# A fused attention and MLP kernel: batch 0 with its scores in sixteens and without filler matmuls, and TensorE in a written-out order from batch 1 on

## The chip, the cores and the metric

The kernel runs on one NeuronCore of a Trainium2 chip. The metric is device time in microseconds (us) of one execution. Seven runs of the kernel before gave a median of 268.73 us (268.46 to 270.62).

The core has five engines that run beside each other and wait for one another by semaphores: TensorE (PE: matmuls, with the weight loads shown as PEld), VectorE (DVE), ScalarE (ACT), GpSimd (POOL) and SyncE (SP). POOL and SP also issue most DMAs. Matmuls write to PSUM; DVE and ACT empty it.

## The reference

For each of 4 batches and 8 heads, a sorting matrix P (8 x 8) mixes the 8 blocks of 96 rows of k and v; each block of q then attends to its own mixed block. The result x (768 x 512 for a batch) goes through a residual MLP with affine norms.

```python
for _ in range(5):                                  # P: (4, 8, 8, 8)
    P = np.exp(P - np.max(P, axis=-1, keepdims=True))
    P = P / (np.sum(P, axis=-1, keepdims=True) + 1e-09)
    P = P / (np.sum(P, axis=-2, keepdims=True) + 1e-09)
k_sorted = np.einsum('bhij,bhjcd->bhicd', P, k_b)   # v_sorted likewise
scores = scale * np.matmul(q_b, k_sb.transpose(0, 1, 2, 4, 3))
attn = softmax(scores)
x = heads side by side of np.matmul(attn, v_sb)     # (4, 768, 512)
a1 = alpha1 * x + beta1
u = x + lam * np.einsum('ts,bsd->btd', w_tok, a1)
a2 = alpha2 * u + beta2
out = u + lam * (np.maximum(a2 @ w_ch1, 0.0) @ w_ch2)
```

## The kernel before

**Stages.** Everything is unrolled. First come five rounds of the normalisation of P on ACT and DVE (lines 234 to 253), with `spin` matmuls on TensorE beside them: products of the identity that nothing reads. Then batch 0's attention with a code of its own, and the transposed token weights (`sort_wtok`, `prep_wtok`). Then for each batch the token mixing (`moe_a`: `tok_part`, `moe_tok`, `moe_turn`) and the MLP in two halves of 384 rows: `moe_h` (16 hidden tiles of 4 matmuls 128x384, ReLU on ACT) and `moe_ch` (three row tiles of 16 matmuls 128x512, then two DVE operations and two stores). A batch's MLP runs beside the next batch's attention.

**Batch 0** (lines 681 to 722). `mix_v0` and `mix_k0` make a head pair's mixed v and k (12 matmuls each, copied out in a part of four and a part of two, one by ACT and one by DVE); `turn_v0` transposes v into `Vs[0]`; `sc0` makes eight score matmuls for half a head pair and one exponential; `pv0` makes 12 matmuls with the values, a reciprocal and a product on DVE. Most `sc0` and the last two `pv0` begin with one or two `spin` matmuls. In this stage every engine keeps the order in which the code issues (`Engine.fixed`).

**Later batches.** `mix_v` and `mix_k` mix v and k for all heads; v takes a trip through DRAM (`vscr`) into `Vs[b % 2]`. `emit_scores` and `emit_pv` work by head pairs h4 = 0 to 3. From line 740 on TensorE and ACT, and from 743 DVE, aren't fixed: a planner puts the instructions in order by priority and a modelled time, except for the piece at lines 759 to 765.

**Buffers.** PSUM pool psA has 2 buffers of two banks (scores, values and mixes of the later batches), psB 4 buffers of one bank (all the rest). The hidden tiles lie in `hTa` and `hTb`, one buffer each for both halves. `ost` (output rows) has 2 buffers, `kT` 2.

**Queues.** POOL issues, in this order: q, v, k of batch 0, the token weights, the affine vectors, `W1p`, v of batch 1, `W2p`, then `prep_affine` and the additions of `moe_start`, then k and q of batch 1. At most eight of its DMAs are under way: the ninth waits for the first to land. SP issues the v trip, the transposes of q (`cross_q`, from batch 2 on) and of u (`moe_turn`, from batch 1 on), and the stores.

Of the kernel before, what the change touches and what calls it, by code (L numbers as in the profile page):

```python
# [16 lines left out]
def kernel(  # L17
# [73 lines left out]
    def const(shape, dtype, name):  # L91
        return wts.tile(shape, dtype, name=name, tag=name)

    ident16 = const([128, 128], F16, "ident16")
    pool.memset(ident16[:], 0.0)
    pool.affine_select(
        out=ident16[:], in_=ident16[:], compare_op=ALU.not_equal, fill=1.0, base=0,
        pattern=[[-1, 128]], channel_multiplier=1,
    )
    ident32 = const([128, 128], FT, "ident32")  # L100

# [7 lines left out]
    def load_raw(b, kv):  # L109
        src = (k, v)[kv]  # L110
        if b == 0:
            raw = att.tile([128, H, 6, D], F16, name=f"raw{kv}", tag=f"raw{kv}", bufs=2)
            for hh in range(2):
                pool.dma_start(
                    raw[:, hh * 4:(hh + 1) * 4, :, :],
                    src[b, hh * 4:(hh + 1) * 4].rearrange("h (p x) d -> p h x d", x=6),
                )
            raw_of[(b, kv)] = raw
            return
        raw = att.tile([128, HB * D], F16, name=f"raw{kv}", tag=f"raw{kv}", bufs=2)  # L120
        for th in range(2):
            pool.dma_start(
                raw[th * 64:(th + 1) * 64, :],
                src[b].rearrange("h (j th t) d -> th (h j) (t d)", j=NB, th=2)[th],
            )
        raw_of[(b, kv)] = raw

    qn_of = {}
    qT_of = {}

    def load_q(b):
        qT_of[b] = att.tile([128, H4, NT, 128], F16, name="qT", tag="qT", bufs=2)
        if b < 2:
            qn = att.tile([128, H, NT, D], F16, name="qn1", tag="qn", bufs=1)
            n = (4, 2)[b]
            for hh in range(n):
                hs = slice(hh * H // n, (hh + 1) * H // n)
                pool.dma_start(qn[:, hs, :, :], q[b, hs].rearrange("h (p kt) d -> p h kt d", kt=NT))
            qn_of[b] = qn
            return  # L140
# [16 lines left out]
    load_q(0)  # L157
    load_raw(0, 1)
    load_raw(0, 0)
    ones16 = const([128, 1], F16, "ones16")  # L160
    pool.memset(ones16[:], 1.0)
    dve.tensor_copy(ident32[:], ident16[:])
    NV = 2
    Vs = []
    for n in range(NV):
        t_ = const([BLK, H * NB, GRP], F16, f"Vs_{n}")
        dve.memset(t_[:, :, D:GRP], 1.0)
        Vs.append(t_)
# [8 lines left out]
    ab2 = att.tile([2 * CT, 128], FT, name="ab2", tag="sel", bufs=2)  # L177
# [3 lines left out]
    pool.dma_start(ab2[0:CT, :], moe_alpha2.rearrange("(c p) -> c p", p=128))  # L181
    pool.dma_start(ab2[CT:2 * CT, :], moe_beta2.rearrange("(c p) -> c p", p=128))
# [13 lines left out]
    def mask(n):  # L196
        if n == 0:
            dve.tensor_reduce(mskj[:], ident16[:].rearrange("p (b j) -> p j b", j=NB), AXX, ALU.add)
# [8 lines left out]
        else:  # L207
            for th in range(2):
# [25 lines left out]
    for it in range(5):  # L234
# [16 lines left out]
        if it > 2:  # L251
            turn_q(0, it - 3, act.copy)
    spin(psb([128, 512], FT, "spin_ps")[:], 7)

    def load_weights():
        for g in range(4):
            pool.dma_start(W1p[:, :, g * 512:(g + 1) * 512], w1v[:, :, g * 512:(g + 1) * 512])
        load_raw(1, 1)
        for g in range(4):
            pool.dma_start(W2p[:, g * 4:(g + 1) * 4, :], w2v[:, g * 4:(g + 1) * 4, :])  # L260
# [40 lines left out]
    def mixing_heads():  # L301
# [10 lines left out]
        for hh in range(2):  # L312
            hs = slice(hh * 4, hh * 4 + 4)
            dve.tensor_tensor(
                bigH[:, hs, :, :],
                rep[:, hs, :].unsqueeze(3).to_broadcast([128, 4, NB, 16]),
                mskt[:].unsqueeze(1).unsqueeze(1).to_broadcast([128, 4, NB, 16]),
                ALU.mult,
            )

# [6 lines left out]
    def mix_v(b, banks=2, groups=range(6), copies=(act.copy, dve.tensor_copy, act.copy)):  # L327
# [5 lines left out]
        for n in groups[::banks]:  # L333
# [19 lines left out]
    def mix_k(b, share=(4, 0, 4), gs=range(3)):  # L353
        raw = raw_of[(b, 0)]
        rhs = bigP[b][:].rearrange("p g i -> p (g i)")
        if b not in kT_of:
            kT_of[b] = att.tile([128, H4 * NB, BLK], F16, name="kT", tag="kT", bufs=2)
# [17 lines left out]
    def mix_heads(kv, h4, out, copies):  # L375
# [3 lines left out]
        for (lo, hi), copy in zip(((0, 4), (4, 6)), copies):  # L379
# [8 lines left out]
            copy(dst[:, lo:hi], mps[:].rearrange("p t (i r) -> p t i r", r=16))  # L388

    def mix_k0(h4):  # L390
        if 0 not in kT_of:
            kT_of[0] = att.tile([128, H4 * NB, BLK], F16, name="kT", tag="kT", bufs=2)
        mix_heads(0, h4, kT_of[0][:, h4 * NB:(h4 + 1) * NB, :], (act.copy, dve.tensor_copy))
# [3 lines left out]
    def mix_v0(h4):  # L397
        vT0.append(moep.tile([128, NB, BLK], F16, name=f"vT_{h4}", tag="u32", bufs=9))
        mix_heads(1, h4, vT0[h4][:], (dve.tensor_copy, act.copy))
# [12 lines left out]
    def emit_scores(b, h4, g, spins=0):  # L412
        kT = kT_of[b]
        qT = qT_of[b]
        blocks = ((0, 1, 2, 6), (3, 4, 5, 7))[g] if b == 0 else range(4 * g, 4 * g + 4)
        sps = psa([128, 2, 4, 128], FT, "sc_ps")
        spin(sps[:, 0, :, :].rearrange("p i x -> p (i x)"), spins)
        for ii, i in enumerate(blocks):
            for h2 in range(2):
                rows = slice(h2 * 64, (h2 + 1) * 64)  # L420
                pe.matmul(
                    sps[0:BLK, h2, ii, 0:BLK], kT[rows, h4 * NB + i, :], qT[rows, h4, :, i * 16:(i + 1) * 16],
                    start=True, stop=True,
                )
        et = att.tile([BLK, 2, 4, BLK], F16, name="et", tag="et", bufs=4)
# [35 lines left out]
    def pv_tiles(h4, g, et, spins=0):  # L461

        bank = psb([128, 4, 128], FT, "x_ps")[:].rearrange("p a x -> p (a x)")
        spin(bank, spins)
        xps = bank[:, 0:6 * GRP].rearrange("p (a i g) -> p a i g", i=3, a=2)
        flat = et[:].rearrange("p a i x -> p (a i x)")
        for rows, i in ((slice(0, 128), 0), (slice(BLK, 128), 3)):
            for h2 in range(2):
                for ii in range(3):
                    vi = 3 * g + ii if i == 0 else 6 + g  # L470
                    at = (h2 * 4 + ii) * BLK
                    lhsT = flat[:, at:at + 128] if i == 0 else et[:, h2, 3, 32 * ii:32 * ii + 32]
                    pe.matmul(
                        xps[rows, h2, ii, 0:D + 1], lhsT, Vs[0][:, (2 * h4 + h2) * NB + vi, 0:D + 1],
                        start=True, stop=True,
# [8 lines left out]
    def emit_attention(b):  # L484
        x128 = moep.tile([128, NT, C], F16, name="x128", tag="x128", bufs=2)
        xs = moep.tile([BLK, 2, C], F16, name="xs", tag="xs", bufs=1)
        x_of[b] = x128

        def gather(lo, hi):
            for a in range(3):  # L490
                dve.tensor_copy(x128[96:128, a:a + 4:3, lo:hi], xs[32 * a:32 * a + 32, :, lo:hi])

        prev = [emit_scores(b, 0, g) for g in range(2)]
        for h4 in range(1, H4):
            cur = [emit_scores(b, h4, g) for g in range(2)]
            emit_pv(b, h4 - 1, prev, x128, xs)
            prev = cur
            if h4 == H4 - 1:
                gather(0, 384)
        emit_pv(b, H4 - 1, prev, x128, xs)  # L500
        gather(384, C)


# [5 lines left out]
    def sort_wtok(n):  # L509
# [3 lines left out]
        for lo, hi, base in ((0, 96, 0), (96, 128, TAIL)):  # L513
            w = hi - lo
            dve.tensor_copy(
# [122 lines left out]
    def moe_h(b, hf, which=range(HT)):  # L638
        if (b, hf) not in hT_of:
            hTa = moep.tile([128, 12, 384], BF, name="hTa", tag="big", bufs=1)  # L640
            hTb = moep.tile([128, HT - 12, 384], BF, name="hTb", tag="hTb", bufs=1)
            hT_of[(b, hf)] = [hTa[:, m, :] if m < 12 else hTb[:, m - 12, :] for m in range(HT)]
        for m in which:
# [6 lines left out]
            act.activation(hT_of[(b, hf)][m], hps[:], AF.Relu)  # L650

    def moe_ch(b, hf, kks=range(3)):
        hT = hT_of[(b, hf)]
        for kk in kks:
# [3 lines left out]
            for lo, hi in ((0, 384), (384, C)) if last else ((0, C),):  # L658
                cps = psb([128, hi - lo], FT, "ch_ps")
                for m in range(HT):  # L660
# [3 lines left out]
                    )  # L664
                dve.tensor_tensor(cps[:], cps[:], lamB[:, lo:hi], ALU.mult)
# [4 lines left out]
                )  # L670

# [3 lines left out]
    def sc0(h4, g, spins=0):  # L675
        ets[(h4, g)] = emit_scores(0, h4, g, spins)

    def pv0(h4, g, spins=0):
        pv_tiles(h4, g, ets[(h4, g)], spins)

    x_of[0] = moep.tile([128, NT, C], F16, name="x128", tag="x128", bufs=2)
    mixing_heads()
    turn_q(0, 2, act.copy)
    mix_v0(0)
    turn_q(0, 3, act.copy)
    for h4 in range(1, H4):
        mix_v0(h4)
    load_weights()
    turn_v0(0, dve.tensor_copy)
    mix_k0(0)  # L690
    mix_k0(1)
    sc0(0, 0, 1)
    turn_v0(1, dve.tensor_copy)
    sc0(0, 1, 1)
    mix_k0(2)
    pv0(0, 0)
    sc0(1, 0, 1)
    turn_v0(2, dve.tensor_copy)
    pv0(0, 1)
    sc0(1, 1, 1)  # L700
    mix_k0(3)
    pv0(1, 0)
    sc0(2, 0, 1)
    sort_wtok(0)
    pv0(1, 1)
    sc0(2, 1, 1)
    sort_wtok(1)
    prep_wtok(range(1), dve.tensor_copy)
    pv0(2, 0)
    sort_wtok(2)  # L710
    sc0(3, 0)
    prep_wtok(range(1, 2), dve.tensor_copy)
    pv0(2, 1)
    sc0(3, 1)
    prep_affine()
    turn_v0(3, act.copy)
    prep_wtok(range(2, 4), act.copy)
    pv0(3, 0, 2)
# [3 lines left out]
    pv0(3, 1, 2)  # L722
# [5 lines left out]
    load_raw(1, 0)  # L728
    load_q(1)
# [18 lines left out]
    moe_h(0, 0, range(5))  # L748
    for n in range(6):
        moe_h(0, 0, range(5 + n, 6 + n))  # L750
# [5 lines left out]
    moe_h(0, 0, range(11, HT))  # L756
    moe_turn(0, 1)
    stack.close()
    pe.fixed = True
    for kk in range(2):  # L760
        moe_ch(0, 0, (kk,))
        mix_k(1, gs=((0, 1), (2,))[kk])
        for h4 in range(2 * kk, 2 * kk + 2):
            turn_q(1, h4, dve.tensor_copy)
    pe.fixed = False
    for b in range(1, B):
        if b > 1:
            if b > 2:
                cross_q(b)
            mixing_matrices(b)  # L770
            mix_v(b)
            if b == 2:
                opened = pool.tensor_copy(gate[:], Vs[0][0:1, 0, 0:2])
                with tc.issue_after(opened.ins):
                    load_q(3)
                    load_raw(3, 1)
                    load_raw(3, 0)
            mix_k(b)
        emit_attention(b)
        if b == 1:  # L780
            moe_ch(0, 0, (2,))
        else:
            moe_h(b - 1, 0)
            moe_ch(b - 1, 0)
        moe_h(b - 1, 1)
        moe_a(b)
        moe_ch(b - 1, 1)
# [3 lines left out]
    for hf in range(2):  # L791
        moe_h(B - 1, hf)
        moe_ch(B - 1, hf)
# [30 lines left out]
```

The softmax here doesn't subtract the row's maximum and nothing guards it: scores larger than these inputs give would overflow.

## Time and profile before

| | |
|---|---|
| median of 7 runs | 268.73 us |
| profiled execution, its own time | 268.85 us |
| its span, first to last instruction | 267.1 us |
| mean granted TensorE clock | 0.998 |
| PE, DVE, ACT, POOL busy | 97%, 58%, 47%, 35% |
| first mixing matmul of batch 0 | 13.10 us |
| first `tok_ps` matmul of batch 0 | 33.97 us |
| first `tok_ps` matmul of batches 1 and 2 | 85.59 us, 144.37 us |

Times within the profile count from the start of the span. A row of the timeline merges instructions of a kind: its start, the stretch that they take, engine, line, operation, output and inputs, shape, and count. All lines read L65, since one helper issues everything; tiles tell the instructions apart. A matmul's end is modelled and overlaps the next one's start, so the pace of TensorE is read from one row's start to the next row's start. "x_ps" are the products with the values, "sc_ps" the scores, "m_ps", "k_ps" and "v_ps" the mixes, "vt_ps" and "q_ps" the transposes of v and q.

### The profile page before, as it was taken

How to read it: one execution, taken by the hardware profiler on the slowest of the kernel's cores; microseconds unless marked ns; L12 is line 12 of the kernel's file. 1: busy time of each engine (PE TensorE's matmuls, PEld its weight loads, DVE VectorE, ACT ScalarE, POOL GpSimd, SP SyncE). 2: the span in 40 equal slices, each digit the busy share in tenths (PEclk: the TensorE clock that was granted, in tenths of full speed). 3: DMA queues.
4: the chain of work that ended last, by engine and by line, in shares of the span. 5: the costliest groups of instructions: out<-in, count | busy, mean ns of one | idle time of the engine just before them, and what ended most of it. 6: DMA issues, size and time to landing. Idle time of an engine off the chain costs nothing.

```text
span 267.1 us, 5149 instructions
## 1 busy us (share of the span) xinstructions
PE 258.6 (97%) x2049; PEld 141.6 (53%) x2059; DVE 154.6 (58%) x333; ACT 125.8 (47%) x232; POOL 92.7 (35%) x100
## 2 busy tenths in 40 slices
PE   7899999999999999999999999999999999999993
PEld 2467745566555444554565444654565445545542
DVE  5878778629567866632675957714585962042033
ACT  3376757643585312880375414970475305604600
POOL 8523689203675624008817225002409000000000
PEclk9999999999999999999999999999999999999999
DMA  5999999999999543499999442495200332012012
GB/s 76 176 208 255 207 212 206 210 214 109 205 180 160 98 93 94 114 94 101 186 205 120 85 98 82 118 91 69 71 11 2 79 78 79 2 39 79 2 39 79
DMA packets 62423, 30.88 MB, mean 116 GB/s; under 512 B 48888, under 2 KB 58112, under 8 KB 62400
## 3 DMA queue, kind: packets, MB, share of 16 engines
q0 software_dynamic: 23024, 15.60, 39.2%
q1 hardware_dynamic: 39280, 14.89, 34.1%
q8 instruction: 16, 0.26, 0.4%
q14 instruction: 7, 0.06, 0.1%
q10 hardware_dynamic: 96, 0.07, 0.1%
HBM read 32.78 MB, written 8.65 MB: 155 GB/s over the span
## 4 chain that ended last, share of the span: by engine, by line
PE 80%; DMA 9%; POOL 3%; ACT 3%; DVE 2%; issue 1%; POOLq 0%; DVEq 0%
PE ch_ps L65 31%; PE h_ps L65 30%; PE tok_ps L65 9%; DMA wt<-in_moe_w_tok_dram 6%; DMA W1p<-in_moe_w_ch_dram 3%; PE sc_ps L65 3%; PE x_ps L65 3%; ACT kT L65 2%; PE v_ps L65 2%; PE k_ps L65 1%; POOL qn L65 1%; POOL raw L65 1%; DVE u L65 1%; PE q_ps L65 1%; DVE tok_ps L65 1%
## 5 line engine op out<-in xcount | busy, mean ns | idle before, releaser
L65 PE MATMUL h_ps<-a2T,W1p 128*128 128x384 bf16 x512 | 93.5, 327 | 0.1
L65 ACT ACTIVATE hTa<-h_ps 128x384 bf16<-128x384 f32 x96 | 45.9, 492 | 68.8 <-PE h_ps L65 67.7
L65 PE MATMUL ch_ps<-W2p,hTa 128*128 128x512 bf16 (+2 forms) x290 | 66.0, 371 | 0.5
L65 PEld LDWEIGHTS <-W1p 128*128 128x128 bf16 x512 | 47.5, 98 | 30.4 <-issue 0.9
L65 DVE TENSOR_TENSOR ch_ps<-ch_ps,lamB 128x512 f32<-128x512 f32 (+2 forms) x25 | 16.9, 676 | 64.0 <-PE ch_ps L65 61.4
L65 POOL TENSOR_SCALAR u<-b1lB,rs 128x512 f32<-128x512 f32 x18 | 28.8, 1609 | 64.4 <-DVE ost L65 58.6
L65 PEld LDWEIGHTS <-hTa 128*128 128x128 bf16 x300 | 28.6, 98 | 32.5
L65 PE MATMUL tok_ps<-x,w_tokT 128*128 128x512 f16 x144 | 32.1, 379 | 0.0
L65 POOL TENSOR_TENSOR u<-x,u 128x512 f32<-128x512 f16 x22 | 25.3, 1181 | 18.2 <-DVE x L65 17.3
L65 ACT ACTIVATE et<-sc_ps 96x768 f16<-96x768 f32 x32 | 24.9, 807 | 11.7 <-PE sc_ps L65 11.7
L65 ACT CAST u<-u 128x512 f16<-128x512 f32 x24 | 14.8, 618 | 24.1 <-DVE u L65 21.7
L65 PE MATMUL ch_ps<-W2p,hTb 128*128 128x512 bf16 (+2 forms) x100 | 25.0, 371 | 0.0
L65 PEld LDWEIGHTS <-w_tokT 128*128 128x128 f16 x180 | 14.8, 97 | 16.1
L65 DVE TENSOR_TENSOR tok_ps<-tok_ps,a1lB 128x512 f32<-128x512 f32 x24 | 16.5, 691 | 7.3 <-PE tok_ps L65 7.3
L65 DVE CAST kT<-k_ps 64x512 f16<-64x512 f32 x24 | 16.5, 687 | 3.4 <-PE k_ps L65 3.0
L65 DVE TENSOR_TENSOR x<-x_ps,recip 96x512 f16<-96x512 f32 (+2 forms) x32 | 17.6, 554 | 0.9
L65 DVE TENSOR_TENSOR u<-tok_ps,u 128x512 f32<-128x512 f32 x24 | 16.3, 688 | 1.7
L65 ACT ACTIVATE hTb<-h_ps 128x384 bf16<-128x384 f32 x32 | 15.3, 497 | 3.8 <-PE h_ps L65 3.4
L65 DVE TENSOR_TENSOR ost<-ch_ps,u 128x512 f32<-128x512 f32 (+2 forms) x25 | 16.6, 664 | 0.6
L65 POOL DMA_DIRECT2D qn<-in_q_dram x18 | 15.4, 872 | 4.2 <-PE q_ps L65 3.4
L65 PEld LDWEIGHTS <-hTb 128*128 128x128 bf16 x100 | 9.6, 98 | 10.9
L65 PEld LDWEIGHTS <-et 96*128 96x128 f16 (+2 forms) x288 | 12.4, 99 | 4.6 <-issue 1.2
(95 smaller groups left out, 216.0 us busy)
## 6 DMA issues: line engine op xcount, KB each, us to landing
out_dram<-ost SPq DMA_DIRECT2D x23, 192.0 KB, 2.2
raw<-in_v_dram POOLq DMA_DIRECT2D x8, 384.0 KB, 9.2
raw<-in_k_dram POOLq DMA_DIRECT2D x8, 384.0 KB, 11.2
vscr<-vA SPq DMA_DIRECT2D x6, 384.0 KB, 4.4
Vs<-vscr SPq DMA_DIRECT2D x6, 384.0 KB, 7.9
W1p<-in_moe_w_ch_dram POOLq DMA_DIRECT2D x4, 512.0 KB, 10.4
W2p<-in_moe_w_ch_dram POOLq DMA_DIRECT2D x4, 512.0 KB, 18.3
qn<-in_q_dram POOLq DMA_DIRECT2D x12, 128.0 KB, 5.8
```

Source lines behind the costliest of these rows:

```text
L65: ins = getattr(self.eng, name)(*args, **kwargs)
```

## The change

**Start.** The first load of q is issued ahead of the identity; k and v of batch 0 come by halves, k first; the two small loads of `ab2` go from POOL to SP; the fill of `Vs` with ones and the copy to `ident32` move from the start into the rounds of P; the last three transposes of q all come in the last round, with five spins behind them for seven, and two more in `mixing_heads`, which makes `bigH` in parts of two and six heads.

**Batch 0.** A loop over head pairs: 16 score matmuls in a row into two psA tiles, then two exponentials, the transposes of v, the values of the head pair before, and the mixes of the next. No spins. ACT takes the larger part of the v copies too, and the last `sort_wtok`. The tail rows of `pv_tiles` come first, written with 128 rows, and the main rows over them.

**POOL's queue.** `prep_affine` comes before the loads of k and q of batch 1, and these before `W2p`, which is issued after the first additions of `moe_start`.

**From batch 1 on.** TensorE is always fixed. `moe_h` and `moe_ch` become generators that yield an amount of time per unit, and `weave` puts so much of them between the steps of the attention; a step is 16 scores or 16 products of values. The two halves' hidden tiles get a buffer each, `kT` has one. For batch 1 the mixes of k and the transposes of q lie between the last tiles of `moe_h(0, 0)`.

```diff
+    load_q0(0)
     ident16 = const([128, 128], F16, "ident16")
...
+    ab2 = att.tile([2 * CT, 128], FT, name="ab2", tag="sel", bufs=2)
+    nc.sync.dma_start(ab2[0:CT, :], moe_alpha2.rearrange("(c p) -> c p", p=128))
+    nc.sync.dma_start(ab2[CT:2 * CT, :], moe_beta2.rearrange("(c p) -> c p", p=128))
+    for h4 in range(1, H4):
+        load_q0(h4)
+    load_raw0(0)
+    load_raw0(1)
...
-        if it > 2:
-            turn_q(0, it - 3, act.copy)
-    spin(psb([128, 512], FT, "spin_ps")[:], 7)
+        if it == 3:
+            turn_q(0, 0, act.copy)
+        if it == 4:
+            for h4 in range(1, H4):
+                turn_q(0, h4, act.copy)
+    spin(psb([128, 512], FT, "spin_ps")[:], 5)
...
         load_raw(1, 1)
+        prep_affine()
+        load_raw(1, 0)
+        load_q(1)
+
+    def load_w2():
         for g in range(4):
             pool.dma_start(W2p[:, g * 4:(g + 1) * 4, :], w2v[:, g * 4:(g + 1) * 4, :])
...
+    def attention_steps(b, first):
...
+        def values(h4):
+            emit_pv(b, h4, ets[h4], x128, xs)
+            if h4 > 1:
+                lo, hi = ((0, 384), (384, C))[h4 - 2]
+                for a in range(3):
+                    dve.tensor_copy(x128[96:128, a:a + 4:3, lo:hi], xs[32 * a:32 * a + 32, :, lo:hi])
+
+        yield 0, lambda: scores(0)
+        yield 2.4, lambda: scores(1)
+        yield first, lambda: values(0)
+        yield 2.2, lambda: scores(2)
+        yield 2.4, lambda: values(1)
+        yield 2.2, lambda: scores(3)
+        yield 2.4, lambda: values(2)
+        yield 2.4, lambda: values(3)
+
+    def weave(fill, steps):
+
+        for gap, step in steps:
+            filled = 0
+            while filled < gap:
+                took = next(fill, None)
+                if took is None:
+                    break
+                filled += took
+            step()
...
-            hTa = moep.tile([128, 12, 384], BF, name="hTa", tag="big", bufs=1)
-            hTb = moep.tile([128, HT - 12, 384], BF, name="hTb", tag="hTb", bufs=1)
+            hT = moep.tile([128, HT, 384], BF, name="hT", tag=("big", "hT1")[hf], bufs=1)
...
             act.activation(hT_of[(b, hf)][m], hps[:], AF.Relu)
+            yield 0.65
...
+                    if m < HT - 1:
+                        yield 0.216
...
+    for h4 in range(H4):
+        sc0(h4)
+        turn_v0(h4, dve.tensor_copy if h4 < 3 else act.copy)
+        if h4 == 3:
+            prep_wtok(range(0, 1), dve.tensor_copy)
+            prep_wtok(range(1, 2), act.copy)
+        if h4 > 0:
+            pv0(h4 - 1, 0)
+            if h4 == 3:
+                sort_wtok(1, dve.tensor_copy)
+            pv0(h4 - 1, 1)
+        if h4 < 3:
+            k_copy, v_copy = mix_k0(h4 + 1), mix_v0(h4 + 1)
+            k_copy(0, act.copy)
+            k_copy(1, dve.tensor_copy)
+            v_copy(0, act.copy)
+            v_copy(1, dve.tensor_copy)
+        if h4 == 2:
+            sort_wtok(0, dve.tensor_copy)
+    sort_wtok(2, act.copy)
...
+    for n in range(3):
+        mix_k(1, gs=(n,))
+        run(moe_h(0, 0, range(10 + 2 * n, 11 + 2 * n)))
+        turn_q(1, n, dve.tensor_copy)
+        run(moe_h(0, 0, range(11 + 2 * n, min(12 + 2 * n, HT))))
+    turn_q(1, 3, dve.tensor_copy)
...
+        if b == 1:
+            fill = chain(moe_h(0, 1), moe_ch(0, 0), moe_ch(0, 1, (0, 1)))
+            steps = [(0.6, lambda: mixing_matrices(2)), (0.6, lambda: mixing_matrices(3)), (0.8, lambda: None)]
+        else:
             if b > 2:
                 cross_q(b)
...
+            fill = chain(moe_h(b - 1, 0), moe_ch(b - 1, 0), moe_h(b - 1, 1), moe_ch(b - 1, 1, (0,)))
+            steps = [
+                (0.0, mixes(b, 0)), (0.0, mixes(b, 1)), (1.8, mixes(b, 2)),
+                (1.8, lambda: mix_k(b, gs=(0,))), (1.8, lambda: mix_k(b, gs=(1,))),
+                (2.4, lambda: mix_k(b, gs=(2,))), (3.0, lambda: None),
+            ]
...
+        weave(fill, steps + list(attention_steps(b, 5.6 if b == 1 else 5.3)))
+        run(fill)
         moe_a(b)
-        moe_ch(b - 1, 1)
+        run(moe_ch(b - 1, 1, (2,) if b == 1 else (1, 2)))
```

## The prediction

> **What bounds the kernel now.** I read the page first, then the busy times by stage, then TensorE's timeline, row by row.
>
> ```profile
> PE 258.6 (97%) x2049; PEld 141.6 (53%) x2059; DVE 154.6 (58%) x333; ACT 125.8 (47%) x232; POOL 92.7 (35%) x100
> ```
> ```profile
> 13.10:33.97 20.87, 19.82 (x384) 15.23 (x384) 16.05 (x37) 14.39 (x23) 9.49 (x13) 1.00 1.21 222
> ...
> 103.90:144.40 40.50, 40.25 (x335) 22.54 (x337) 22.21 (x47) 24.02 (x45) 17.27 (x19) 1.00 1.12 128
> 144.40:162.40 18.00, 17.95 (x84) 8.06 (x83) 12.87 (x24) 4.21 (x8) 5.82 (x6) 1.00 0.48 102
> ```
> The columns of the second are the stretch, its length, then PE, PEld, DVE, ACT, POOL. TensorE never rests after batch 0, so from 34 us on time can only come from matmuls that cost more than their stream. In batch 0 its 19.82 us are partly spins; there DVE is busy 77% and ACT 69% of the time, which is where a limit will appear once the spins are gone.
>
> The start (TensorE):
> ```profile
> 1.35 6.14 PE L65 MATMUL spin_ps<-ident 128*128 128x512 f16 x16 [1.35 <-POOL ident L65]
> ...
> 9.36 1.68 PE L65 MATMUL spin_ps<-ident 128*128 128x512 f16 x7
> 11.47 0.34 PE L65 MATMUL pj_ps<-ident,P 32*8 32x8 f16 x8 [0.42 <-DVE P L65]
> ```
> Sixteen spins take 6.1 us, the last seven 0.22 each: the array is slow at first. P arrives at 11.41 and TensorE has waited 0.4 us for it.
>
> One turn of batch 0, with its spin of 0.32 us (20.48 to 20.80):
> ```profile
> 20.48 0.39 PE L65 MATMUL sc_ps<-ident 128*128 128x512 f16 x1
> 20.80 0.38 PE L65 MATMUL sc_ps<-qT,kT 64*96 64x96 f16 x8
> 21.11 0.65 PE L65 MATMUL vt_ps<-ident,vT 128*96 128x128 f16 x8
> 21.59 0.63 PE L65 MATMUL x_ps<-Vs,et 96*128 96x65 f16 x12
> 22.16 0.39 PE L65 MATMUL sc_ps<-ident 128*128 128x512 f16 x1
> ```
> Scores of batch 2, in eights and a fifteen:
> ```profile
> 115.99 0.56 PE L65 MATMUL sc_ps<-qT,kT 64*96 64x96 f16 x15
> 116.47 0.66 PE L65 MATMUL h_ps<-a2T,W1p 128*128 128x384 bf16 x3
> ...
> 117.57 0.50 PE L65 MATMUL h_ps<-a2T,W1p 128*128 128x384 bf16 x2
> 118.00 0.38 PE L65 MATMUL sc_ps<-qT,kT 64*96 64x96 f16 x8
> 118.31 1.48 PE L65 MATMUL h_ps<-a2T,W1p 128*128 128x384 bf16 x8
> 119.62 2.75 PE L65 MATMUL ch_ps<-W2p,hTa 128*128 128x512 bf16 x11
> ```
> Eight h take 1.31, so 0.164 each; the two at 117.57 take 0.43, 0.10 too much. Eight scores take 0.31, fifteen 0.48: a further pair costs 0.049, so a group has 0.11 of fixed cost. Breaking h for a group of scores costs 0.21 us.
>
> The end of an attention, on DVE (duration min/median/max, then the three last copies):
> ```profile
> L65 DVE COPY x<-xs x6: 219/354/1112, 81.3 to 84.6; 32x768 f16<-32x768 f16 x3, 32x256 f16<-32x256 f16 x3
> ...
> 84.09 1.61 DVE L65 COPY x<-xs 32x256 f16<-32x256 f16 x3
> ```
> The last copy takes 1.11 in place of 0.22 us: POOL's addition began beside it at 84.46.
>
> **The change part by part** (the profiled execution: span 267.1, own time 268.85, 0.12 above the median).
>
> *Start: +0.35.* The load ahead of the identity takes POOL about 0.85 us, so spins begin at 2.2. If the array speeds up at 6.65 as now, 16 spins end at 7.9; q0 (0.6), three spins (0.65), three transposes of q (0.5 each, the last landing near 10.0 now at 10.22) and five spins end near 12.0. P itself is later by about 0.4 (the copy to ident32, 0.23, and two memsets, 0.3, fall into DVE's pauses, which now fit with 0.03 to spare): 11.8. So pj comes at 12.1 for 11.47; but bigH's first part is short (0.36 for 0.68) and q no longer lies in between: the first mix at 13.45 for 13.10. ab2 on SP: nothing there waits, and POOL saves two issues that wait 1.4 us each.
>
> *Batch 0: -1.0.* I follow the three queues with durations of this stage: DVE steps 0.61 (Vs copy), 0.69 (reciprocal and product), 0.42 (k, quarter), 0.75 (sort_wtok), 0.50 (w_tokT); ACT 0.72 (exp), 0.57 and 0.95 (kT, Vs), 0.75 (w_tokT); 0.2 from TensorE to a reader, 0.1 back. sc0(0) at 14.55, held by the k copies, then 17.2 (bigH's second part, 1.0 on DVE). A full round: scores 0.65, transposes 0.45, latency 0.3, Vs copy 0.61, two products 1.38, k copy 0.42, latency 0.1: 3.9. So 21.1 and 25.0. The rest: DVE's sort, copies and products end at 32.95, ACT's exps, Vs, sort_wtok(2) (1.6, estimated from its copies of 256, 512 and 768 columns at 0.37, 0.58, 0.81) and three w_tokT at 32.2. First tok_ps at 33.3 for 33.97. TensorE has slack throughout, so its ten spins (2.8 us) and four saved groups of scores bring nothing themselves. With start: -0.65. Bounds: ACT's work alone (14.39 less two q copies, plus 1.2 and 1.6) ends near 29.6, -4; with no overlap between DVE operations and the array fast only at 8 us, +1.5. The pv_tiles form costs the same 12 matmuls.
>
> *Token mixing of batch 0: -0.3.* prep_affine leaves the tail of POOL's waits (its second product ends at 35.36, and DVE and ACT wait for it at 35.41); TensorE's gap at 41.12 behind ACT's u (0.33) goes.
>
> *POOL's and SP's loads: 0.* At 1.93 us per 384 KB and 2.5 per 512 KB (the landings of k of batch 0 and of W2p lie so far apart now), k of batch 1 lands by 45 (needed at 50.5), q by 47 and 49 (needed from 51.7), W2p, issued from 40 on behind four additions, by 59 (needed at 71, since moe_h(0, 1) now goes first). The v trip of batch 1 took 15.8 us from issue: 50 + 15.8 = 66 against values at 71; of batch 2, 13.8 against 19.6. If a cover were 5 us short, that would be TensorE's wait.
>
> *Buffers: 0.* With one kT, the k copies of a batch wait for the last scores of the batch before, over 20 us earlier; with a hidden buffer for each half, moe_h of the second half no longer waits for moe_ch of the first. One kT too few would cost the 2.7 us of a k copy.
>
> *k and q of batch 1: +0.4.* Four single q groups at 0.6 for two doubles at 0.93, and two more switches.
>
> *Scores in sixteens, batches 1 to 3: -2.6.* Eight groups per batch become four: 12 x 0.21. Values in sixteens save under 0.1.
>
> *Small waits of batches 2 and 3: -1.0.* By the starts, h rows ahead of v, k and scores are 0.15 to 0.22 too long at 107.1, 109.1, 110.1, 112.6 and 116.5: 0.9 per batch. The mixes now have 1.95 of h between them, against copies of 1.0 to 1.2 (2.7 on DVE for k, two buffers). Half of it I count.
>
> *New wait, batches 2 and 3: +1.2.* By the yields, 10 units of moe_ch are left behind values(3): 2.2 us. From the start of values(3) TensorE reaches tok at 2.8; DVE needs 2.2 for its products and 0.25, 0.25 and 1.1 for the copies: 3.9. The third of the products of tok reads the last copy, at 3.25: a wait of 0.6. Today 4 to 5.5 us of h lie there. Queued behind it are all later matmuls. Batch 1 has 4.3 us and no wait.
>
> *Other covers.* a2T of batch 1 came 10.6 us after the first tok; now needed at 7.8 + 3.5 + 0.9 = 12.1 (slack 1.5), later ones at 14.7 or more. Between steps: two exps and a ReLU end 2.4 after scores begin, against 3.4; DVE's products 2.2 against 3.15, or 3.5 with a moe_ch ending in front.
>
> Sum: -0.65 - 0.3 + 0.4 - 2.6 - 1.0 + 1.2 = -3.0. From the median, 265.7.
>
> **A rule against it.** Between the seventh spin at 10.66 and pj at 11.47 TensorE stood for 0.8 us, and the transposes after that still had their full pace. My longest gap without spins is 0.75. The Trainium skill ("TensorE: Matmul & The Clock Gate", section "A second HAM failure mode: psum-queue depth-cycling") says otherwise: many short idles between groups can make the clock fall to half and recover again and again; its Part 4 adds that transposes don't count as activity. By the row the sum is 265.7. By the rule, batch 0's work of 15.6 us (8 x 0.31 scores, 4 x 0.48, 8 x 0.57, 8 x 0.46 mixes, 3.0 for the weights) would grow by 4 to 11 with the array slow, say 7: 272.7. I take the row, and keep the rule as a rival.
>
> **The rivals.**
> *The clock falls in batch 0* (0.08): slower, 272.7, as worked out. For it: nothing reads the spins, so they were only activity. Against it: the 0.8 us pause. It decides once more than 3 us are lost there.
> *The written order waits as much as it saves* (0.13): ACT and DVE are still put in order by the planner, whose times aren't the chip's; 0.12 us at each of 24 steps takes the 3 us: 268.7, 267 to 270. The point is DVE's 3.5 against 3.15 behind values.
> *SP is late* (0.05): the six transposes of q for batch 2 (7.1 us for five) fall between u and a2T of batch 1; less 1.5 of slack, 270.5.
> *Batch 0 shrinks as far as ACT allows in part* (0.15): another -2.5, 263.
> *As summed* (0.59): 264 to 267.3.
>
> **How the numbers follow.** A measurement of this kernel can tell about 0.5%, 1.3 us: faster below 267.4, slower above 270.1. Faster: 0.55 of the summed case, 0.15, and 0.02 of the written order: 0.72. Same: 0.04, 0.09 and 0.01: 0.14. Slower: 0.08, 0.04 and 0.02: 0.14. The range from 263.0 to 269.3 leaves out the clock, most of SP and the best of batch 0.
>
> **What would show it.** Right: scores in groups of 16 only, tok_ps of batch 0 first near 33.3, a gap of about 0.6 inside the first tok group of batches 2 and 3 behind DVE's x, no other wait over 0.3. Wrong: matmuls of 128x512 near 0.43 apart after 14 us; a wait on psA at each step; a gap at the first h of batch 1; tok_ps of batch 0 before 31.5 or after 35.

## The result and the profile after

The changed kernel takes 271.46 us (median of 15 executions, 269.77 to 280.79; one more on record took 268.75), the kernel before 268.76 us (36 executions). The ratio is 1.0081, 95% interval 1.0061 to 1.0101. Medians are over all executions named with them, while ratios and intervals compare only executions within 1.5% of the fastest of their kernel, here 9 of the 16. The changed kernel is slower by about 1%; the prediction had 265.7 with a range up to 269.3. The profiled execution of the changed kernel is at the median, 271.46 us, with a span of 269.7 (before 267.1), so the rows below show the usual loss: 2.6 us.

The page, engine totals and the granted clock in 40 slices of 6.7 us:

```profile
PE 255.8 (95%) x2034; PEld 144.3 (53%) x2049; DVE 155.2 (58%) x331; ACT 127.4 (47%) x234; POOL 90.5 (34%) x98
PEclk9999658999999999999999999999999999999999
```

TensorE has less to do (255.8 for 258.6 us) although part of it ran at half speed: the slices from 27 to 47 us have a clock of 0.5 to 0.8. Before, the mean clock was 0.998.

Batch 0 and the stretch behind it by windows (stretch, length, then busy us of PE, PEld, DVE, ACT, POOL, granted clock, DMA share, GB/s):

```profile
14.21:37.99 23.78, 19.33 (x362) 17.03 (x363) 16.61 (x35) 15.41 (x23) 9.28 (x12) 0.80 1.19 222
37.99:60.00 22.01, 21.99 (x145) 11.67 (x142) 17.33 (x32) 13.57 (x26) 12.66 (x11) 0.90 1.13 193
```

Batch 0 from the first mix to the first tok_ps takes 23.78 us for 20.87, at a clock of 0.80 for 1.00, without any spins in it. The start, on TensorE's timeline:

```profile
2.82 6.21 PE L65 MATMUL spin_ps<-ident 128*128 128x512 f16 x16 [2.82 <-POOL ident L65]
...
12.75 0.34 PE L65 MATMUL pj_ps<-ident,P 32*8 32x8 f16 x8
```

The identity comes 1.47 us later (2.82 for 1.35) and the first mix 1.11 (14.21 for 13.10). The end of batch 0, all engines, idle time in brackets:

```profile
24.89 1.25 POOL L65 DMA_DIRECT2D raw<-in_v_dram  x2 [0.34 <-DMA wt<-in_moe_w_tok_dram]
...
25.59 3.19 DVE L65 COPY wtp<-wt 128x1152 f16<-128x1152 f16 x2
...
25.88 0.65 PE L65 MATMUL vt_ps<-ident,vT 128*96 128x128 f16 x8
26.15 1.28 POOL L65 TENSOR_TENSOR a1lB<-a1lB,lamB 128x512 f32<-128x512 f32 x1
...
27.38 1.27 POOL L65 TENSOR_TENSOR b1lB<-b1lB,lamB 128x512 f32<-128x512 f32 x1
...
28.83 1.46 PE L65 MATMUL wtok_ps<-ident,wtp 128*128 128x128 f16 x12 [2.31 <-DVE wtp L65]
```

`sort_wtok(0)`'s two copies take 3.19 us together and end at 28.78, just behind the two products of `prep_affine` on POOL (26.15 to 28.65); TensorE waits 2.31 us for them. Then the array is slow: twelve transposes take 1.46 us, where the same twelve take 0.84 at full speed (in port_spin, below). The trace's record of the granted clock has it at one half from 28.56 to 42.21 us. The first tok_ps comes at 37.99 for 33.97.

TensorE's waits over the whole span (total, times, longest):

```profile
PE wtok_ps L65 <- DVE wtp L65: 2.9, 2, 2.3
PE spin_ps L65 <- POOL ident L65: 2.8, 1, 2.8
PE tok_ps L65 <- DVE x L65: 1.4, 2, 0.7
```

Behind batch 0 the prediction's gain is there in this execution. From the first tok_ps to the end it takes 269.7 - 37.99 = 231.7 us for 233.1, although four of those microseconds ran at half clock. A stretch of batch 2, and DVE's last copies ahead of its tok_ps:

```profile
139.53 2.77 PE L65 MATMUL h_ps<-a2T,W1p 128*128 128x384 bf16 x16
142.22 0.56 PE L65 MATMUL sc_ps<-qT,kT 64*96 64x96 f16 x16
142.71 2.77 PE L65 MATMUL h_ps<-a2T,W1p 128*128 128x384 bf16 x16
...
148.95 2.33 PE L65 MATMUL ch_ps<-W2p,hT 128*128 128x512 bf16 x10
151.11 0.59 PE L65 MATMUL tok_ps<-x,w_tokT 128*128 128x512 f16 x2
```
```profile
150.75 1.61 DVE L65 COPY x<-xs 32x256 f16<-32x256 f16 x3
```

Sixteen scores take 0.49 from start to start, eight took 0.31 before. The tok_ps of batches 2 and 3 meet the three copies and wait 0.7 us each, as predicted.

### The profile page after: what moved, and what is told of

It reads as the page before. It is cut to its first block, busy times and chain, and to the rows that moved or that the text cites. A ratio compares the mean times of both kernels' runs of the same rounds, so it can differ in the third digit from the quotient of the medians.

```text
span 269.7 us, 5125 instructions
## 1 busy us (share of the span) xinstructions
PE 255.8 (95%) x2034; PEld 144.3 (53%) x2049; DVE 155.2 (58%) x331; ACT 127.4 (47%) x234; POOL 90.5 (34%) x98
## 4 chain that ended last, share of the span: by engine, by line
PE 89%; DVE 7%; issue 1%; ACT 1%; POOL 0%; DVEq 0%; POOLq 0%
PE h_ps L65 31%; PE ch_ps L65 29%; PE tok_ps L65 12%; PE spin_ps L65 3%; PE x_ps L65 3%; DVE x L65 3%; PE sc_ps L65 3%; PE q_ps L65 2%; PE wtok_ps L65 2%; PE k_ps L65 1%; PE v_ps L65 1%; DVE wtp L65 1%; ACT et L65 1%; DVE Vs L65 1%; PE uT_ps L65 0%
## 5 line engine op out<-in xcount | busy, mean ns | idle before, releaser
L65 PE MATMUL h_ps<-a2T,W1p 128*128 128x384 bf16 x512 | 89.9, 327 | 0.0
L65 PE MATMUL ch_ps<-W2p,hT 128*128 128x512 bf16 (+2 forms) x385 | 85.8, 371 | 0.7
L65 ACT ACTIVATE hT<-h_ps 128x384 bf16<-128x384 f32 x128 | 60.0, 492 | 47.5 <-PE h_ps L65 47.0
L65 PEld LDWEIGHTS <-W1p 128*128 128x128 bf16 x512 | 48.5, 98 | 32.2 <-issue 0.3
L65 PEld LDWEIGHTS <-hT 128*128 128x128 bf16 x400 | 37.6, 98 | 41.0
L65 POOL TENSOR_TENSOR u<-x,u 128x512 f32<-128x512 f16 x22 | 25.3, 1182 | 35.8 <-DVE x L65 29.7
L65 PE MATMUL tok_ps<-x,w_tokT 128*128 128x512 f16 x144 | 34.6, 397 | 1.4 <-DVE x L65 1.4
L65 DVE RECIPROCAL recip<-x_ps 96x8 f32<-96x8 f32 (+1 forms) x32 | 6.2, 195 | 30.9 <-PE x_ps L65 30.9
L65 PEld LDWEIGHTS <-et 96*128 96x128 f16 (+1 forms) x288 | 13.6, 114 | 2.4
L65 PE MATMUL x_ps<-Vs,et 96*128 96x65 f16 (+1 forms) x288 | 14.1, 207 | 0.1
L65 PE MATMUL spin_ps<-ident 128*128 128x512 f16 x26 | 8.9, 501 | 2.8 <-POOL ident L65 2.8
```

What stands on the lines that cost most here:

```text
L65: ins = getattr(self.eng, name)(*args, **kwargs)
```

## The experiments

The theory: POOL's products block DVE's copy, TensorE's pause lets the clock fall, and the rest is as summed. The rivals: the missing spins lowered the clock; the written order waits as much as it saves; a queue is late in some executions. "Clock" is the mean granted clock of an execution.

**Taking the collision away (aff_late).**

```diff
-        prep_affine()
         load_raw(1, 0)
         load_q(1)
+        prep_affine()
```

> The changed kernel with prep_affine behind the loads of k and q of batch 1 on POOL, so that its two products run near 33 us and not beside the first sort_wtok on DVE. Theory 1 (the products lock DVE's copy out, TensorE then stands 2.3 us, and its clock falls to half for some 13 us): the second copy of sort_wtok(0) takes 0.25 us for 2.83, the gap before the first wtok_ps goes, the clock stays full, first tok_ps near 34.5 for 37.99, time near 265.8 for 271.5. Theory 2 (the short idles of a batch 0 without spins throttle the clock in any case): the copy is short, but the clock falls between 15 and 40 us all the same, and the time stays above 268.

The copies are short (min, median, max ns), the clock is full through batch 0, and the first tok_ps comes at 32.59.

```profile
L65 DVE COPY wtp<-wt x4: 253/394/450, 25.2 to 28.3; 128x1152 f16<-128x1152 f16 x2, 128x384 f16<-128x384 f16 x2
```

Yet the median is 274.98 us (270.16 to 276.16, 4 executions; the profiled one is 275.46). So batch 0 was not the whole of it; here the loss appears in batch 1:

```profile
66.93 23.80 SPq L140 DMA_TRANSPOSE qT<-qn  x6
90.83 0.52 SPq L709 DMA_DIRECT2D out_dram<-ost  x1
```
```profile
93.63 0.69 DVE L65 TENSOR_TENSOR ost<-ch_ps,u 128x512 f32<-128x512 f32 x1 [7.10 <-DMA out_dram<-ost]
...
94.97 0.65 PE L65 MATMUL x_ps<-Vs,et 96*128 96x65 f16 x8 [6.24 <-DVE x L65]
```

The first fence is SP's timeline, the second DVE's and TensorE's. The six transposes of q for batch 2 stand on SP ahead of batch 0's stores; they hold SP for 23.8 us, where six with their inputs there take 7.86 (in q2_aff, below). The profile puts 6.1 us of that down to waits for the q loads; the rest is open. The first store is issued at 90.83. `ost` has two buffers, so DVE stands 7.1 us at the third row tile; behind it in DVE's queue are batch 1's values, whose PSUM buffers TensorE needs: 6.2 us, and the clock fell again (92.6 to 99.4). In the kernel before only one transpose stood ahead of these stores, and the other five behind them:

```profile
71.39 1.34 SPq L149 DMA_TRANSPOSE qT<-qn  x1
74.69 0.32 SPq L667 DMA_DIRECT2D out_dram<-ost  x1
75.06 0.43 SPq L668 DMA_DIRECT2D out_dram<-ost  x1
82.57 7.06 SPq L149 DMA_TRANSPOSE qT<-qn  x5
```

**The collision in the kernel before (before_aff).**

```diff
         load_raw(1, 1)
+        prep_affine()
         for g in range(4):
             pool.dma_start(W2p[:, g * 4:(g + 1) * 4, :], w2v[:, g * 4:(g + 1) * 4, :])
...
     sc0(3, 1)
-    prep_affine()
     turn_v0(3, act.copy)
```

> The kernel before with one move: prep_affine right behind the load of v of batch 1, ahead of W2p on POOL. Theory 1 (POOL's products lock DVE's wide copies out): a copy of sort_wtok takes 1.3 to 2.6 us more than its 0.25 to 0.8, TensorE waits there, and the time rises by 1 to 2.5, more if the clock falls in the gap. Rival (the copy in the changed kernel was long for another reason, such as the weights' landing): no copy above 0.8 us, time 268.0 to 269.0.

272.95 us (271.32 to 274.94), ratio 1.0165 [1.0101, 1.0229]. One `sort_wtok` copy takes 2847 ns here, TensorE's wait is below, and the clock is at half from 32.3 to 35.8. This one move makes the old kernel slower by 4.1 us, spins and all.

```profile
PE wtok_ps L65 <- DVE w_tokT L65: 2.2, 1, 2.2
```

**Only the spins (before_nospin)**: the kernel before without the ten spins of batch 0's steps.

```diff
-    sc0(0, 0, 1)
+    sc0(0, 0)
     turn_v0(1, dve.tensor_copy)
-    sc0(0, 1, 1)
+    sc0(0, 1)
...
-    pv0(3, 1, 2)
+    pv0(3, 1)
```

> The kernel before without the ten spins in the steps of batch 0. Theory 1 (short idles do not lower the clock; only a pause of 2 us and more does): clock full, and DVE and ACT set the pace, 268.0 to 268.8. Theory 2 (the spins carry the clock): it falls to half between 15 and 40 us, 270 to 275.

269.16 us (268.07 to 270.36, 12 executions), ratio 1.0016 [0.9999, 1.0032]. The clocks are 0.986 to 1.0, against 0.992 to 1.0 for the kernel before beside it: without spins the clock does fall a little in some executions. But the interval leaves it 0.3% at most, and q2_aff (below) keeps 0.999 or more with no spins in batch 0 either, so the rival of the spins falls as the main cause. In the profiled execution (clock 0.998) the first tok_ps comes 1.33 us sooner:

```profile
32.64 4.04 PE L65 MATMUL tok_ps<-x,w_tokT 128*128 128x512 f16 x18
```

So the spins were not free in batch 0. The span is 267.1 us all the same: 0.94 us goes in waits for batch 0's u, and where the rest goes is open.

**Filling the pause (spin_gap)**: the changed kernel with eleven spins where TensorE stood.

```diff
         turn_v0(h4, dve.tensor_copy if h4 < 3 else act.copy)
         if h4 == 3:
+            spin(psb([128, 512], FT, "spin_ps")[:], 11)
```

> The changed kernel with eleven spins between the transposes of v of the last head pair and the first wtok_ps; prep_affine stays beside sort_wtok. Theory 1: the copy still takes 2.8 us, but TensorE is busy through the gap, the clock stays full, first tok_ps near 36.5, time near 268. Theory 2 (short idles everywhere): the clock falls all the same, time near 271.

271.35 us (268.24 to 277.49, 12 executions), ratio 1.0004 [0.9986, 1.0023] of the kernel before. The profiled execution keeps the full clock: 268.26 us, first tok_ps at 34.79. Executions at 0.998 or more take 268.2 to 270.2, those at 0.981 to 0.994 take 272.5 to 277.5. The clock holds in these 6 of 12 executions, while the highest of the changed kernel is 0.993. Yet even there nothing is gained on the kernel before: TensorE waits 1.7 us for DVE's x and xs in batch 1, and DVE, ahead of them, for the stores:

```profile
DVE ost L65 <- DMA out_dram<-ost: 2.1, 1, 2.1
```

The copy took 1420 ns in this execution, so the long pause was not there to be filled.

**Only the order (weave_only)**: the start, batch 0 and spins of the kernel before, `prep_affine` at its old place, the order of the loads and all from batch 1 on as changed (score groups, buffers, generators and `weave`).

```diff
         load_raw(1, 1)
+        load_raw(1, 0)
+        load_q(1)
+
+    def load_w2():
         for g in range(4):
...
-    def emit_attention(b):
+    def attention_steps(b, first):
...
+    def weave(fill, steps):
```

> The start and batch 0 of the kernel before (spins, order of loads of q, k and v, prep_affine at its old place) with everything behind batch 0 from the changed kernel: the loads of k and q of batch 1 ahead of W2p, TensorE in the written order, a hidden buffer for each half. Theory 1 (the written order is a gain that batch 0 hides): first tok_ps at 34.0, clock full, 231.7 less the 2.1 us that the slow clock took behind it, so about 3.5 less than before: 265.2, with waits of 0.7 at tok of batches 2 and 3. Rival (the written order gains nothing, and the 1.4 us seen behind tok_ps is chance): 268 to 269.

274.52 us (269.29 to 279.02, 11 executions), ratio 1.0061 [1.0017, 1.0106]. TensorE's waits:

```profile
PE x_ps L65 <- DMA Vs<-vscr: 3.9, 1, 3.9
```

The v trip is late: POOL issues the q loads of batch 2 at 60.8, while the trip is under way. The clock falls here too, from 77.52 to 80.93. So written order and queues together lose without any collision in batch 0; ten of the eleven executions have a clock below 0.997.

**The work for q of batch 2 put in its place (q2_only, q2_sp, q2_pool).** q2_sp has the first two changed places below, q2_pool the last two, q2_only all four.

```diff
-                nc.sync.dma_start(out[b, kt * 96:(kt + 1) * 96, lo:hi], ost[0:96, lo:hi])
+                stores[(b, kt)] = nc.sync.dma_start(out[b, kt * 96:(kt + 1) * 96, lo:hi], ost[0:96, lo:hi])
...
-        with tc.issue_after(regroup[b - 1].ins):
+        with tc.issue_after((stores[(0, 2)] if b == 2 else regroup[b - 1]).ins):
...
     load_raw(2, 0)
+    raw2 = pool.last
...
-            load_q(2)
+            with tc.issue_after(raw2.ins):
+                load_q(2)
             cross_q(2)
```

> The changed kernel with the loads of q of batch 2 behind those of k and v of batch 2 on POOL, and its six transposes on SP behind the third pair of stores and no longer ahead of the first; prep_affine stays beside sort_wtok. Theory (two causes: POOL's products lock DVE's copy in batch 0, and on SP the transposes wait for loads while the stores, so the two output buffers, so DVE, so the values of batch 1, wait behind them): the waits of TensorE between 70 and 100 us for DVE's x and for the v trip go, the clock still falls near 28 us, median 269 to 270 for 271.5, and fewer runs above 272. Rival (all of the spread is batch 0's clock): same median and spread as the changed kernel.

264.67 us (263.58, 264.22, 265.11 and 269.32), ratio 0.9828 [0.9791, 0.9864]. The collision is still there, and the profiled execution, the one of 269.32, shows it: copy 2828 ns, clock at half from 29.2 to 36.1, first tok_ps at 38.07; no wait in batch 1. The two executions at a clock of 1.0 are the two shortest. The median is below the 269 to 270 expected, since three of the four did not lose what the profiled one lost; what the collision did in them isn't traced.

> The changed kernel with the six transposes of q of batch 2 on SP behind the third pair of stores; their loads stay early on POOL, ahead of those of k and v, and prep_affine stays. If the order on SP is the cause behind batch 0: no wait of DVE for out_dram, values of batch 1 at most 1 us late for the v trip (the early loads still share the DMA engines with it), 264 to 267 with one run in four near 269 (the clock). If the early loads are the cause: as the changed kernel, 270 to 272.

268.32 us (265.29 to 271.7, 9 executions), ratio 0.9933 [0.99, 0.9967]. The stores are issued from 79.4 on, but in the profiled execution x_ps waits 1.9 us for `Vs`: the early loads are a cause as well.

> The changed kernel with the loads of q of batch 2 behind those of k and v on POOL, while the transposes on SP stay ahead of most stores. If the order on SP is the cause: the transposes wait for loads that now come even later, so the stores, DVE and the values of batch 1 wait longer, 272 to 280. If the early loads are the cause: 264 to 267.

266.3 us (265.24 to 278.89, 20 executions), ratio 0.9911 [0.9892, 0.9931]. I had expected 272 to 280: a miss. With the loads late, the planner itself put only two transposes ahead of the first stores (80.24 to 82.84) and four behind, so this edit mends part of SP's order too. Each half is worth some microseconds; they are not additive, and I can't divide the sum between them.

**Both causes away (q2_aff)**: q2_only with `prep_affine` as in aff_late.

> Both mends: prep_affine behind the loads of k and q of batch 1, and q of batch 2 late as in q2_only. Theory of two causes: no wait of TensorE above 1 us, clock full, first tok_ps near 32.6, 265 to 266 in most runs. Rival (the written order of TensorE waits by itself whatever the queues do): the wait moves to another operand of the values of batch 1, and the time stays above 268.

265.51 us (265.19 to 266.1), ratio 0.9875 [0.9849, 0.9901], with clocks of 0.999 to 1.0. That is 3.1 us below the kernel before; the prediction's sum was 3.0, but some of its terms miss in opposite directions (below). The copies of `sort_wtok` by DVE (min, median, max ns), in the changed kernel and in q2_aff:

```profile
L65 DVE COPY wtp<-wt x4: 254/450/2826, 25.6 to 32.2; 128x1152 f16<-128x1152 f16 x2, 128x384 f16<-128x384 f16 x2
```
```profile
L65 DVE COPY wtp<-wt x4: 253/376/450, 25.4 to 28.6; 128x1152 f16<-128x1152 f16 x2, 128x384 f16<-128x384 f16 x2
```

SP's timeline now has the stores first and the transposes unhindered, 7.86 us for six:

```profile
78.03 0.33 SPq L711 DMA_DIRECT2D out_dram<-ost  x1
...
87.01 7.86 SPq L140 DMA_TRANSPOSE qT<-qn  x6
```

**The order alone, mended (weave_q2)**: weave_only with the edits of q2_only.

> The kernel before with its own start, batch 0 and spins, then the changed kernel's order from batch 1 on, and with the q loads of batch 2 behind raw(2) on POOL and their transposes behind the store of (0, 2) on SP. Theory (the written order is worth what I summed for it, about -2.6 -1.0 +1.2 +0.4 -0.3 = -2.3, once the q work of batch 2 is out of the way): 266.5, from 265.5 to 267.5; no wait for Vs or for x in batch 1; first tok near 35 as in weave_only, so up to 1.1 of it may be given back. Rival A (the order itself waits as much as it saves, and the gain of the mended kernels comes from the shorter batch 0): 268.3 to 269.5. Rival B (what made weave_only slow is not the q work): x_ps still waits 3 to 4 us for Vs, and 271 or more.

265.94 us (265.53 to 266.21), ratio 0.9893 [0.987, 0.9917]: 2.7 us faster than the kernel before, where weave_only was slower. The only wait left behind batch 0 is the predicted one; the 1.6 us for P lie in the start:

```profile
PE pj_ps L65 <- DVE P L65: 1.6, 1, 1.6
PE tok_ps L65 <- DVE x L65: 1.4, 2, 0.7
```

From the first tok_ps to the end it takes 264.4 - 34.72 = 229.7 us for 233.1. So all that changed from batch 1 on (order, buffers, loads) is worth 3.4 us, and the q work took it away.

**The collision alone (port_spin)**: q2_only with the spins of spin_gap.

> The changed kernel with the q work of batch 2 mended and prep_affine where the change put it, but eleven spins in the pause that sort_wtok(0) leaves in TensorE. It parts the price of the collision on the port from the price of the clock's fall. Theory (two prices): the spins keep the clock at full speed in most executions, and what is left is the late first tok, near 34.8 as in spin_gap for 32.9 with prep_affine behind: 265.5 to 267, with every run at a clock of 0.995 or more below 267.5. Rival A (spins between do not keep the clock): clock 0.975 to 0.99 in most runs and 267 to 270. Rival B (the collision costs nothing by itself, the copies catch up): 263.5 to 264.7.

265.87 us (265.82 to 266.44), ratio 0.9899 [0.9871, 0.9927], with clocks of 0.997 to 0.999. TensorE's timeline:

```profile
25.81 2.54 PE L65 MATMUL spin_ps<-ident 128*128 128x512 f16 x11
...
30.89 0.84 PE L65 MATMUL wtok_ps<-ident,wtp 128*128 128x128 f16 x12 [0.97 <-DVE wtp L65]
```

The first tok_ps comes at 34.54 for 32.88 in q2_aff, so collision and spins together cost 1.7 us. In q2_only's profiled execution, with the long copy and the clock's fall, it comes at 38.07. But here POOL's products began at 25.60 and the copy took only 1616 ns: it ended at 27.01, before the spins did. So this trace does not show spins that fill a pause of 2.3 us. That spins hold the clock is likely (four of four executions at 0.997 or more), not shown: without spins, 16 of the 33 executions of q2_only, q2_sp and q2_pool had such a clock as well.

**Towards a better version.** q2_aff still waits 1.1 us for u in batch 0, since its `prep_affine` comes late. q2_aff_ident is q2_aff with the first load of q behind the identity:

```diff
-    load_q0(0)
     ident16 = const([128, 128], F16, "ident16")
...
+    load_q0(0)
     ident32 = const([128, 128], FT, "ident32")
```

> q2_aff with the identity made before the first load of q is issued. Theory: the first spin at 1.4 for 2.8 us, P's use near 11.8 for 12.3, and the rest 0.5 to 1.1 earlier: 264.5 to 265.3. Rival (the array's clock speeds up later [...], and the loads are later): no more than 0.2 from q2_aff.

265.84 us (265.43 to 267.21), ratio 0.9894 [0.9858, 0.993]. Spins begin at 1.35, tok_ps at 31.84, and 2.5 us of waits for u take it all back. mid therefore is q2_aff_ident with `prep_affine` between the two loads of q of batch 1 (`load_q` now calls it there):

```diff
-        prep_affine()
         load_raw(1, 0)
-        load_q(1)
+        load_q(1, prep_affine)
```

> q of batch 2 late on both queues, the identity first, and prep_affine between the two loads of q of batch 1, so that it runs near 30 us, when DVE makes no copy of the weights, and b1lB is ready before rs. Expected: first tok_ps near 31.9, TensorE's waits for ACT's u (2.5 us in the variant with prep_affine last) gone, clock full: 263.3 to 264.3. Rival (some DVE copy still meets a product of POOL, or the pause before wtok_ps trips the clock): 265.5 or more.

263.48 us (263.18 to 264.05), ratio 0.9801 [0.9782, 0.9821]; the first tok_ps at 32.11, no wait for u. mid_tok puts one row tile of `moe_ch` more ahead of tok_ps of batches 2 and 3:

```diff
-            fill = chain(moe_h(b - 1, 0), moe_ch(b - 1, 0), moe_h(b - 1, 1), moe_ch(b - 1, 1, (0,)))
+            fill = chain(moe_h(b - 1, 0), moe_ch(b - 1, 0), moe_h(b - 1, 1), moe_ch(b - 1, 1, (0, 1)))
...
-        run(moe_ch(b - 1, 1, (2,) if b == 1 else (1, 2)))
+        run(moe_ch(b - 1, 1, (2,)))
```

> mid, and in batches 2 and 3 two row tiles of moe_ch, not one, put between the steps of the attention, so one and not two behind the token mixing. The wait of 0.7 us at tok of batches 2 and 3 was predicted from the copies of xs: with 3.5 us more cover it goes, 1.4 less than mid, 262 to 263. Rival: a2T of the batch is then needed 3.5 us sooner (slack 1.5 us by the prediction), and a wait before the first h of the next batch gives the 1.4 back.

261.6 us (261.48 to 261.8), ratio 0.9728 [0.9712, 0.9745], a clock of 0.999 in the profile: the best version, 7.2 us below the kernel before and 1.9 below mid, for the 1.4 expected. Its totals and its longest waits, with tok_ps gone from them:

```profile
PE 250.5 (96%) x2034; PEld 140.8 (54%) x2049; DVE 152.4 (59%) x331; ACT 127.1 (49%) x234; POOL 90.7 (35%) x98
```
```profile
PE spin_ps L65 <- POOL ident L65: 1.4, 1, 1.4
PE sc_ps L65 <- DVE kT L65: 0.5, 2, 0.3
```

## Why the prediction was wrong

*POOL's and SP's loads: 0.* This is the step that failed, twice. It asked whether each moved transfer lands before it is needed, and not what a moved item does to its neighbours. First, `prep_affine` is no transfer, and the sum counted only what its move takes from the end of batch 0 (-0.3): at its new place its products run beside DVE's copies. I had read such a case in the trace of before (a copy of 1.11 us for 0.22 beside POOL's addition) and used it only where it already stood. The Trainium skill says the same ("SBUF — State Buffer", "Who interferes with whom": a DVE copy and a POOL instruction can exclude each other from a shared port, for the whole instruction of the first). 2826 ns for some 250 agree with the blocking; the copy's record begins 0.2 us ahead of POOL's, though, and still it lasts through both products. Secondly, the step did not follow the q work of batch 2: loads on POOL during the v trip, transposes on SP ahead of the stores. aff_late shows the chain, q2_aff against aff_late its price: the one execution of aff_late that kept its clock (0.999) took 270.16, 4.7 us more than q2_aff's median. The other three, whose clock fell, took 274.5 to 276.2.

*SP is late (0.05).* It named the right six transposes and the wrong victim. Not a2T waited, but the stores, then `ost`, DVE and the values. Its 270.5 was near the result by luck: by its own figures (7.1 less 1.5, on 265.7) it should have been 271.3, and it was only one cause of two.

*A rule against it, and the clock in batch 0 (0.08).* The row chosen, the 0.8 us pause, holds nearly for short idles: before_nospin shows it, with its small loss of clock. What failed is "my longest gap is 0.75": the collision made one of 2.31. The condition "more than 3 us lost" could not see that a single pause suffices.

*Token mixing of batch 0: -0.3.* `prep_affine` does leave the end of batch 0, but any place trades: ahead of the copies it collides, behind all loads u waits (1.1 in q2_aff). Of the places tried only mid's does neither.

*Start: +0.35* was +1.1 for the first mix: the load holds POOL's identity for 1.47 us, not 0.85.

*Batch 0: -1.0.* Without the collision (q2_aff) the first tok_ps comes at 32.88 for the predicted 33.3. That is near by luck: the first mix is 0.97 us later than before, not 0.35, and batch 0 from there takes 2.06 us less, not 1.0. The working put the ten spins at nothing; before_nospin shows 1.33 us for them alone.

*Scores, small waits, k and q, new wait: -2.0 together* (-2.6 - 1.0 + 0.4 + 1.2). weave_q2 measured -3.4 behind the first tok_ps. The new wait was 0.7 each for 0.6. So the other terms gave -4.8 for -3.2; I did not part them.

In the profiled execution the loss adds up: +4.0 at the first tok_ps, -3.4 from the order, and about 2.1 of half clock behind 37.99 (4.2 us at half speed), in sum +2.7 for the measured +2.6. Against the prediction it is +4.7 at the first tok_ps (37.99 for 33.3), +2.1, and -1.1 for an order worth 3.4 and not 2.3 (the 2.0 above and 0.3 for token mixing): +5.7, and 271.46 is 5.8 above 265.7. The q work costs nothing in that execution: its row tiles come later than in aff_late, by 5.4 us at the first tok_ps, and its first store is issued sooner, at 86.86 for 90.83. It costs 1.7 us of waits in spin_gap, where the first tok_ps comes at 34.79, and 6.2 in aff_late, at 32.59. So in this execution one cause hid the other; what the longer executions of the changed kernel lost wasn't profiled.

The q work alone is enough to keep the kernel from its gain: none of the executions of aff_late and weave_only is below 269.29. So is the collision where it is long and the clock falls: all four executions of before_aff (271.32 to 274.94), and 269.32 for q2_only's profiled one. But the other three of q2_only, whose products stand at the same place, gain 3.5 to 5 us.

## What to carry to other kernels

Of a step that is moved to another place in a queue, list what runs beside it there, not only when its result is needed: a POOL operation beside a DVE copy can be a wait, and a transpose ahead of stores a wait of whoever fills the output buffers. A planner that places DMAs by modelled times has to be checked in the trace of each new order; two explicit dependencies were worth 2.8 us here between the executions that kept their clock (spin_gap at 0.998 or more, median 268.7, to port_spin, 265.87), and more where late stores also cost the clock. When an experiment mends one cause and the time stays, look for a second that the first one hid.

## What the runs showed of the hardware that I had not expected

One pause of TensorE can be enough for the clock. A wait of 2.3 us in batch 0 came with half speed for 13.65 us (the changed kernel), 6.83 (q2_only) and 10.24 (q2_pool), one of 2.2 with 3.41 (before_aff), one of 3.9 with 3.41 (weave_only) and one of 6.2 with 6.83 (aff_late): all multiples of 3.41. A wait of 1.9 us (q2_sp, for `Vs`) was not followed by any. Yet one of 1.64 in the start of weave_q2 was, 2.8 us after its end and with only idles of up to 0.3 us between; the second row is a window, with the clock of 0.50 third from the end:

```profile
11.46 0.34 PE L65 MATMUL pj_ps<-ident,P 32*8 32x8 f16 x8 [1.64 <-DVE P L65]
```
```profile
14.23:17.64 3.41, 3.41 (x53) 2.99 (x50) 2.11 (x5) 1.82 (x4) 0.52 (x1) 0.50 1.28 212
```

So the length of a wait alone does not decide. The Trainium skill ("TensorE: Matmul & The Clock Gate", "Why this matters for your kernels") warns of gaps over about 3 us; here less sufficed. Why the length of the slow stretch differs between executions is open.

The collision varies too, because `prep_affine` stands behind loads that wait for the token weights to land (the bracket of POOL's row at 24.89). Its first product began at 26.15 in the changed kernel, 25.60 in port_spin and 27.02 in q2_sp, where it missed the first pair of copies and hit the second (1385 ns). That fits a wide spread of these kernels, though the q work spreads them too: weave_only, with no collision, took 269.29 to 279.02. In mid_tok, where neither cause is left, it is 261.48 to 261.8.
